# A SwiGLU feed-forward on one core: whole-array matmuls in the opening stage, fewer junk matmuls, and the first weight sums split by matrix

## The chip, the cores and the metric

The kernel runs on 1 core of one Trainium2 chip. The metric is the device time of one execution in microseconds; of several runs the median counts. The profile is that of one execution, whose instructions and DMA packets are given in microseconds from the start of its span.

## What is computed

```python
def reference(x, w_gate, w_up, w_down):
    g = silu(x @ w_gate)
    u = x @ w_up
    return (g * u) @ w_down
```

All tensors are bf16: x is 2048 tokens by D = 512, w_gate and w_up are 512 by F = 1376, w_down is 1376 by 512. F is ten tiles of 128 and a remainder of 96.

## The kernel before

**Stages.** The 2048 tokens are four chunks c of 512. The first stage makes, for each F tile `ft` and chunk, a gate and an up product in PSUM (4 matmuls over D, or 8 of half the columns), takes the silu of the gate on ScalarE and the product h on VectorE. The second multiplies h by w_down. Most of both is done in a Strassen-like scheme: blocks of two F tiles by two chunks (a unit) take 7 instead of 8 block products, on sums of weights (S1 to S4) and sums of x (T1 to T4) that are made ahead, and PSUM results are put together by VectorE and POOL. The rest is "classic": F tiles 0-3 of chunk 0 (lines 688-701), the same tiles of chunk 1 (`early`, lines 1014-1023; F tile 3 at line 1047), and the remainder of F (`plan_x`, `plan_y`, lines 1037-1044).

**Order on TensorE** at the start: 6 warm-up matmuls; transposes of tokens 0-255; junk matmuls (`between`, line 395), which read a constant and write a bank that nothing reads; gates of F tiles 0-3 for tokens 0-511, in pieces as weights and tokens land; ups of these (line 700); the early tiles 0, 1, 2 of tokens 512-1023; then the remainder: `plan_x` for chunks 0 and 1, `plan_y` for both, `plan_x` for chunks 2 and 3, `plan_y`; then the first unit, the early tile 3, and the other units.

**Halves and whole.** `gu_emit` (line 421) issues each step over D as two matmuls, one for each half of 64 columns of the array, side by side. `gu_whole` (line 433) issues it as one of 128 columns. `gu_group` (line 443) and `classic` (line 470) choose: `classic` takes the whole array where banks are handed to it (`own`).

**Loads.** All loads are issued on SP's queue in the order of lines 282-321: x of tokens 0-255 (`xn`), gate weights of F tiles 0-3 (`wg0`, `wg2`), x of tokens 256-511 (`x0b`, a transposing DMA), up weights of F tiles 0-3 (`wu0`, `wu2`), x of tokens 512-767 and 768-1023 (`x1a`, `x1b`, transposing), weights of F tiles 4, 5 and of 8 to the end, x of chunks 2 and 3, weights of 6, 7, and w_down.

**The planner.** Work on TensorE and SP has a fixed order. Work on ScalarE (A), VectorE (D) and POOL (G) is ordered by `Plan.schedule` (lines 59-103): again and again the operation that can start earliest goes next, ties going to the lower priority number. It reckons with costs that are written in the code and, for loads, with dates of landing (`.land`, line 259): the sum of the loads' sizes so far, plus 300 ns where this is under 10000, else plus 1600. Each engine then runs its list in order and waits on semaphores, so an operation that waits holds back those behind it.

**Sums.** `w_sums(0, ...)` (line 1015) makes the weight sums of F tiles 0 and 1 on POOL: four instructions, each for gate and up together, so they wait for both weights. `x_sums(0, "D", ...)` makes T1 to T4 of tokens 0-1023 on VectorE, one behind the other, T1 behind the last of the weight sums; the weight sums of the units follow T4 on POOL.

**Banks.** PSUM has 8 banks. The gates of chunk 0 take 0-3, the ups 4-7; the early tiles take (0, 2), (1, 3), (4, 5); `plan_x` of chunks 0, 1, 2, 3 takes 6, 7, 5, 2; `plan_y` takes 4 and 3. So `plan_x` of chunk 2 waits until the product h of early tile 2 has read bank 5.

Of the kernel before, what the change touches and what calls it, by code (L numbers as in the profile page):

```python
# [5 lines left out]
ALU = mybir.AluOpType  # L6
BF16 = mybir.dt.bfloat16
FP32 = mybir.dt.float32
# [1 line left out]

N_WARM = 6
N_FILL = 1
N_BETWEEN = 5

PE_STEP, PE_STEP4, PE_LAG = 216, 231, 205
A_BUSY, A_LAG = 485, 180
# [152 lines left out]
def bass_standalone__swiglu_ffn__prompt_kernel(nc, x, w_gate, w_up, w_down, out):  # L169
    _, S, D = x.shape  # L170
    F = w_gate.shape[1]
    P = 128
    KD = D // P
    KH = KD // 2
# [3 lines left out]
    SC = 512  # L178
# [6 lines left out]
    HT = SC // 2  # L185
    HC = P // 2
    NXN = HT // P
    NB = 8
# [8 lines left out]
    XC0 = NFF * P  # L197

    with ExitStack() as es:
# [7 lines left out]
        w_sb = sb("w_sb", [P, KD, 2, WW], BF16)  # L207
# [18 lines left out]
        psum = ps("psum", [P, NB, 512], FP32)  # L226
# [19 lines left out]
        ones_w = nc.const_aps.tensor(1.0, [P, P], BF16)  # L246
        ones_m = nc.const_aps.tensor(1.0, [P, SC], BF16)
        zero_c = nc.const_aps.tensor(0.0, [P, 4], FP32)

        plan = Plan()  # L250
        engines = {"P": nc.tensor, "S": nc.sync, "A": nc.scalar, "D": nc.vector, "G": nc.gpsimd}

        landed = 2700

        def load(name, emit, writes, busy, lag):
            nonlocal landed
            landed += lag
            i = take(homes[name] if name in homes else rest[0])
            plan.add("S", emit, writes=writes, busy=busy, lag=1800, dma=(i, 16)).land = landed + (300 if landed < 10000 else 1600)

        slabs = [(0, 2), (2, 4), (4, 6), (6, 8), (8, NFF + 1)]
        slab_of = {ft: a for a, b in slabs for ft in range(a, b)}
# [73 lines left out]
        def tt_op(engs, out, a, b, alu, reads, writes, prio, busy, after=()):  # L336
            return plan.add(
                engs, lambda e: e.tensor_tensor(out, a, b, alu), reads, writes, busy,  # L338
                G_LAG if engs == "G" else D_LAG, prio, after=after,
            )  # L340
# [5 lines left out]
        def pe(emit, reads, writes, n, step=PE_STEP, after=()):  # L346
            return plan.add("P", emit, reads, writes, int(n * step), PE_LAG, dma=None, after=after)
# [37 lines left out]
        for dk in range(KD):  # L385
            keys = [("b", 2 * dk), ("b", 2 * dk + 1)] if dk < KD - 1 else [("b", 6)]
# [6 lines left out]
            copy_op("DA"[dk % 2], out, src, keys, [("x0a", dk)], 0, 300)  # L393

        def between(e):
            for i in range(N_BETWEEN):
                for h in (0, HC):
                    ins = e.matmul(
                        psum[h:h + HC, NB - 1, 0:P], lhsT=ones_w[:, 0:HC], rhs=ones_m[:, 0:P],
                        start=True, stop=True, tile_position=(0, h),  # L400
                    )
            return ins

        pe(between, (), [("b", NB - 1)], N_BETWEEN / 4)

        n_group = 0

        def next_bank():
            nonlocal n_group
            b = turn[n_group % NB]  # L410
            n_group += 1
            return b
# [8 lines left out]
        def gu_emit(m, ft, c, b, dks, n0, n1):  # L421
            def emit(e):
                for dk in dks:
                    for h in (0, HC):
                        ins = e.matmul(  # L425
                            psum[h:h + HC, b, n0:n1], lhsT=w_sb[:, dk, m, ft * P + h:ft * P + h + HC],
                            rhs=xT_sb[:, dk, c * SC + n0:c * SC + n1], start=(dk == 0), stop=(dk == KD - 1),
                            tile_position=(0, h),
                        )
                return ins  # L430
            return emit
# [33 lines left out]
        def classic_out(ft, c, bg, bu):  # L465
            sg, ksg = ring("sg", sg_sb)
            silu_op(sg, bank(bg), [("b", bg)], [ksg])
            tt_op("D", hview(ft, c), sg, bank(bu), ALU.mult, [ksg, ("b", bu)], [("h", ft, c)], 5, D_BUSY)

        def classic(c, fts, own=None):  # L470
            gates = [next_bank() for ft in fts] if own is None else own[:1]
            ups = [next_bank() for ft in fts] if own is None else own[1:]
            for ft, b in zip(fts, gates):
                gu_group(0, ft, c, b, own is not None)
            for ft, b in zip(fts, ups):
                gu_group(1, ft, c, b, own is not None)
            for ft, bg, bu in zip(fts, gates, ups):
                classic_out(ft, c, bg, bu)
# [4 lines left out]
            return (0, 64) if c % 2 == 0 else (64, 128)  # L483

        def plan_x(c, b):
            def emit(e):
                for dk in range(KD):
                    for m in (0, HC):
                        ins = e.matmul(  # L489
                            psum[m:m + HC, b, :], lhsT=w_sb[:, dk, 0, XC0 + m:XC0 + m + HC],  # L490
                            rhs=xT_sb[:, dk, c * SC:(c + 1) * SC],
                            start=(dk == 0), stop=(dk == KD - 1), tile_position=(0, m),
                        )
                return ins
            pe(emit, x_keys(c) + [f"wg{slab_of[NFF]}", "wut"], [("b", b)], KD)
            y0, y1 = yblk(c)
            sgx, kx = sgx_sb[c % 2], ("sgx", c % 2)
            silu_op(sgx[96:128, :], psum[64:96, b, :], [("b", b)], [kx], 4, 610)
            silu_op(sgy_sb[c // 2][y0:y1, :], psum[0:64, b, :], [("b", b)], [("sgy", c)], 4, 610)
            tt_op(  # L500
                "D", htx_sb[R * c:R * (c + 1), :], sgx[96:128, :], psum[96:128, b, :], ALU.mult,
                [kx, ("b", b)], [("htx", c)], 4, D_BUSY,
            )
            if c == LC:
                tt_op(
                    "D", hl_sb[2 * R:3 * R, :], sgx[96:128, SC - P:SC], psum[96:128, b, SC - P:SC], ALU.mult,
                    [kx, ("b", b)], [("hl", 2)], 4, 300,
                )
# [34 lines left out]
                reads, writes, busy, A_LAG if eng == "A" else G_LAG, prio, after=after,  # L543
            )

        def w_sums(u, prio, after, casts):

            f0, f1 = 2 * u * P, (2 * u + 1) * P
            slot = len(slot_of) % NSLOT
            slot_of[u] = slot  # L550
            block = lambda k, f: w_sb[:, k * KH:(k + 1) * KH, :, f:f + P].rearrange("p k m c -> p m k c")
            at = lambda n: ss_sb[:, slot, W_SUM[n], :, :, :]
            keys = lambda n: [("ss", slot, n, m) for m in range(2)]
            wkeys = [f"w{g}{slab_of[2 * u]}" for g in "gu"]
            for n in ("S1", "S2", "S3", "S4"):
                A11, A12, A21, A22 = (block(k, f) for f in (f0, f1) for k in range(2))
                rd = lambda n: at(n).bitcast(FP32)
                a, b, alu, of_ = {
                    "S1": (A21, A22, ALU.add, ()), "S2": (rd("S1"), A11, ALU.subtract, ["S1"]),
                    "S3": (A11, A21, ALU.subtract, ()), "S4": (A12, rd("S2"), ALU.subtract, ["S2"]),  # L560
                }[n]
                last = tt_op("G", at(n), a, b, alu, wkeys + [k for o in of_ for k in keys(o)], keys(n), prio, 1180, after)
            for m in range(2):
                cast_op(
                    casts, at("A22")[:, m], w_sb[:, KH:2 * KH, m, f1:f1 + P], [wkeys[m]], [("ss", slot, "A22", m)], 8, 360,
                    after if casts == "G" else () if slot < 3 else [last],
                )
            return [last]
# [121 lines left out]
        ups = [NB // 2 + ft for ft in first]  # L690
# [6 lines left out]
        for ft in first:  # L697
            pe(gu_emit(0, ft, 0, gates[ft], range(KD), HT, SC), ["x0b", f"wg{slab_of[ft]}"], [("b", gates[ft])], 2)
        for ft in first:
            gu_group(1, ft, 0, ups[ft])  # L700
            classic_out(ft, 0, gates[ft], ups[ft])

        F_ORDER = [ft for u in U_ORDER[1] for ft in (2 * u, 2 * u + 1)]
# [308 lines left out]

        units = [(pi, u) for pi in range(2) for u in U_ORDER[pi]]
        early = [2 * u + i for u in range(NFF // 2) if u not in U_ORDER[0] for i in range(2)]
        sums = w_sums(0, 8, (), "A")
        g, u = next_bank(), next_bank()
        for h in range(2):
            for m, b in ((0, g), (1, u)):
                emit = gu_emit(m, early[0], 1, b, range(KD), h * HT, (h + 1) * HT)
                pe(emit, [f"x1{'ab'[h]}", f"w{'gu'[m]}{slab_of[early[0]]}"], [("b", b)], KD / 2)  # L1020
        classic_out(early[0], 1, g, u)
        for ft in early[1:3]:
            classic(1, [ft])
        sums = x_sums(0, "D", 4, sums)
        for u in U_ORDER[0]:
            sums = w_sums(u, 2, sums, "A")
        sums = x_sums(1, "G", 2, sums)
# [20 lines left out]
        for n in range(len(units)):  # L1048
# [4 lines left out]
            if n + 1 < len(units):  # L1053
                after = make(n + 1)
# [41 lines left out]
```

## Time and profile before

| | us |
|---|---|
| median of the runs | 115.34 |
| lowest and highest of 3 runs | 114.77, 115.77 |
| the profiled execution | 115.92 |
| its span, first to last instruction | 114.6 |

| engine | busy us | share | instructions |
|---|---|---|---|
| PE (TensorE matmuls) | 111.6 | 97% | 692 |
| PEld (weight loads, beside matmuls) | 69.9 | 61% | 692 |
| DVE (VectorE) | 77.0 | 67% | 113 |
| ACT (ScalarE) | 63.6 | 55% | 123 |
| POOL | 61.5 | 54% | 57 |

How to read it: the chain of waits starts at the last instruction and goes back, at each step, to what released it or to the instruction before it on its engine; its rows give start, length and what ran. A timeline row gives start, length, engine, line of the code, operation, what it writes and reads, the shape, and in brackets the idle time before it with what ended that. `DMA x<-y` is the landing of a load. A windows row gives, for one stretch, its length, the busy time and the number of instructions of PE, PEld, DVE, ACT and POOL, the granted TensorE clock, the busy share of the 16 DMA engines and the GB/s that started in it. A share counts each packet with its whole time where it starts, so it can be over 1. Lines such as L338 are helpers that many operations share: what is written (h_sb, tt_sb, ss_sb) tells them apart.

### The profile page before, as it was taken

How to read it: one execution, taken by the hardware profiler on the slowest of the kernel's cores; microseconds unless marked ns; L12 is line 12 of the kernel's file. 1: busy time of each engine (PE TensorE's matmuls, PEld its weight loads, DVE VectorE, ACT ScalarE, POOL GpSimd, SP SyncE). 2: the span in 40 equal slices, each digit the busy share in tenths (PEclk: the TensorE clock that was granted, in tenths of full speed). 3: DMA queues.
4: the chain of work that ended last, by engine and by line, in shares of the span. 5: the costliest groups of instructions: out<-in, count | busy, mean ns of one | idle time of the engine just before them, and what ended most of it. 6: DMA issues, size and time to landing. Idle time of an engine off the chain costs nothing.

```text
span 114.6 us, 1847 instructions
## 1 busy us (share of the span) xinstructions
PE 111.6 (97%) x692; PEld 69.9 (61%) x692; DVE 77.0 (67%) x113; ACT 63.6 (55%) x123; POOL 61.5 (54%) x57
## 2 busy tenths in 40 slices
PE   7999999999999999999999999999999999999993
PEld 2784854446685857677685858654344556866452
DVE  0104799984866839493957769499999957486423
ACT  5344477774878897767678786740576960000000
POOL 1008701999999999997999999975000000000000
DMA  3999999998000000000000000000041002227966
GB/s 85 261 241 105 260 294 245 221 357 232 10 0 0 3 0 3 6 0 0 0 0 0 3 0 0 6 0 0 0 136 46 0 6 46 46 46 182 200 192 205
DMA packets 22809, 9.84 MB, mean 86 GB/s; under 512 B 12849, under 2 KB 22673, under 8 KB 22801
## 3 DMA queue, kind: packets, MB, share of 16 engines
q1 hardware_dynamic: 20656, 8.69, 33.8%
q10 hardware_dynamic: 2144, 1.05, 3.2%
q8 instruction: 5, 0.08, 0.3%
q14 instruction: 4, 0.02, 0.1%
HBM read 4.75 MB, written 2.10 MB: 60 GB/s over the span
## 4 chain that ended last, share of the span: by engine, by line
PE 90%; DMA 4%; SPq 3%; DVE 1%; issue 0%
PE psum L611 32%; PE psum L724 15%; PE psum L623 12%; PE psum L862 10%; PE psum L425 8%; DMA w_sb<-in_w_up_dram 4%; PE psum L874 4%; PE psum L489 3%; PE psum L752 3%; PE psum L515 2%; PE psum L436 2%; SPq L279 1%; SPq L267 1%; DVE o_sb L327 1%; SPq L284 0%
## 5 line engine op out<-in xcount | busy, mean ns | idle before, releaser
L611 PE MATMUL psum<-tt_sb,ss_sb 128*128 128x512 f32 x160 | 40.0, 403 | 0.0
L611 PEld LDWEIGHTS psum<-tt_sb,ss_sb 128*128 128x128 f32 x160 | 29.9, 188 | 7.5 <-DVE psum L327 0.3
L338 DVE TENSOR_TENSOR ts_sb<-r_sb,psum 128x512 f32<-128x512 f32 x32 | 20.6, 682 | 14.7 <-ACT r_sb L326 14.7
L338 POOL TENSOR_TENSOR h_sb<-sg_sb,ts_sb 128x512 bf16<-128x512 f32 x16 | 20.9, 1311 | 2.2 <-ACT sg_sb L333 2.2
L338 DVE TENSOR_TENSOR h_sb<-sg_sb,psum 128x512 bf16<-128x512 f32 x24 | 16.4, 684 | 6.5 <-PE psum L425 6.1
L326 ACT ACTIVATE r_sb<-psum 128x512 f32<-128x512 f32 x32 | 17.3, 596 | 5.4 <-PE psum L611 5.4
L338 POOL TENSOR_TENSOR ss_sb<-w_sb 128x512 fp32r<-128x512 bf16 x10 | 11.4, 1162 | 14.4 <-DMA w_sb<-in_w_up_dram 7.9
L333 ACT ACTIVATE sg_sb<-psum 128x512 f32<-128x512 f32 x24 | 14.1, 600 | 8.2 <-PE psum L611 5.4
L724 PE MATMUL psum<-wd_sb,h_sb 128*128 128x512 bf16 (+2 forms) x100 | 18.4, 337 | 0.0
L623 PE MATMUL psum<-xT_sb,w_sb 128*128 128x512 bf16 x64 | 15.4, 381 | 0.0
L724 PEld LDWEIGHTS psum<-wd_sb,h_sb 128*128 128x128 bf16 x100 | 8.3, 98 | 9.2 <-issue 1.0
L425 PE MATMUL psum<-xT_sb,w_sb 128*64 128x256 bf16 (+1 forms) x160 | 12.7, 319 | 0.2 <-DMA w_sb<-in_w_up_dram 0.2
L333 ACT ACTIVATE sg_sb<-ts_sb 128x512 f32<-128x512 f32 x16 | 10.2, 636 | 2.2 <-DVE ts_sb L338 2.2
L425 PEld LDWEIGHTS psum<-xT_sb,w_sb 128*64 128x64 bf16 x160 | 8.8, 112 | 3.7 <-DMA w_sb<-in_w_up_dram 0.4
L623 PEld LDWEIGHTS psum<-xT_sb,w_sb 128*128 128x128 bf16 x64 | 5.5, 98 | 8.0 <-issue 2.5
L327 DVE COPY psum<-psum 128x512 f32<-128x512 f32 x8 | 5.6, 699 | 0.9 <-PE psum L623 0.2
L338 POOL TENSOR_TENSOR ss_sb<-w_sb,ss_sb 128x512 fp32r<-128x512 bf16 x5 | 5.9, 1171 | 0.2
L338 POOL TENSOR_TENSOR ss_sb<-ss_sb,w_sb 128x512 fp32r<-128x512 f32 x5 | 5.8, 1168 | 0.0
L327 DVE CAST o_sb<-psum 128x512 bf16<-128x512 f32 (+2 forms) x6 | 3.0, 512 | 4.2 <-PE psum L724 3.1
L338 POOL TENSOR_TENSOR ss_sb<-wd_sb 128x640 fp32r<-128x640 bf16 x4 | 5.6, 1427 | 0.0
L862 PE MATMUL psum<-tt_sb,ss_sb 128*128 128x512 f32 x20 | 5.6, 417 | 0.0
L862 PE MATMUL psum<-th_sb,ss_sb 128*128 128x512 f32 x20 | 5.5, 411 | 0.0
(72 smaller groups left out, 122.0 us busy)
## 6 DMA issues: line engine op xcount, KB each, us to landing
wd_sb<-in_w_down_dram SPq DMA_DIRECT2D x1, 1280.0 KB, 9.1
w_sb<-in_w_gate_dram SPq DMA_DIRECT2D x4, 256.0 KB, 3.9
w_sb<-in_w_up_dram SPq DMA_DIRECT2D x4, 256.0 KB, 4.7
out_dram<-o_sb SPq DMA_DIRECT2D x7, 128.0 KB, 1.8
out_dram<-xT_sb ACTq DMA_DIRECT2D x4, 128.0 KB, 2.5
out_dram<-xT_sb ACTq DMA_DIRECT2D x2, 256.0 KB, 3.3
w_sb<-in_w_gate_dram SPq DMA_DIRECT2D x1, 352.0 KB, 4.5
w_sb<-in_w_up_dram SPq DMA_DIRECT2D x1, 320.0 KB, 5.0
```

What stands on the lines that cost most here:

```text
L326: return e.activation(out, src, ACT.Copy)
L327: return e.tensor_copy(out, src)
L333: "A", lambda e: e.activation(out, src, ACT.Silu), reads, writes, busy, A_LAG, prio
L338: engs, lambda e: e.tensor_tensor(out, a, b, alu), reads, writes, busy,
L425: ins = e.matmul(psum[h:h + HC, b, n0:n1], lhsT=w_sb[:, dk, m, ft * P + h:ft * P + h + HC], rhs=xT_sb[:, dk, c * SC + n0:c * SC + n1], sta ...
L489: ins = e.matmul(psum[m:m + HC, b, :], lhsT=w_sb[:, dk, 0, XC0 + m:XC0 + m + HC], rhs=xT_sb[:, dk, c * SC:(c + 1) * SC], start=(dk == 0), ...
L611: ins = e.matmul(bank(dst), lhsT=s[:, k, :], rhs=t[:, k, :], start=(start and k == 0), stop=(k == KH - 1), skip_group_check=True,)
L623: ins = e.matmul(bank(dst), lhsT=w_sb[:, k0 + k, m, f:f + P], rhs=xT_sb[:, k0 + k, c:c + SC], start=(start and k == 0), stop=(k == KH - 1) ...
L724: ins = e.matmul(psum[:, b, 0:c1 - c0], lhsT=hrows(F_ORDER[n], t, 0, P), rhs=wd_sb[:, F_ORDER[n], c0:c1], start=(start and n == n0), stop= ...
L752: ins = e.matmul(bank(b), lhsT=lhsT, rhs=rhs, start=(start and n == 0), stop=(n == 2 and (kind == "T" or not start)), tile_position=(r0, 0 ...
L862: ins = e.matmul(bank(dst), lhsT=self.ds[s][:, j, self.q, :], rhs=self.dt[t][:, j, :], start=(start and n == 0), stop=(n == NFF // 2 - 1), ...
L874: ins = e.matmul(bank(dst), lhsT=wd_sb[:, 2 * j + a, d * P:(d + 1) * P], rhs=h0_sb[:, 2 * j + a, 0:SC], start=(n == 0), stop=(n == NFF // ...
```

## The change

1. The junk between transposes and gates is one pair of 512 columns and one of 128, instead of five pairs of 128.
2. The ups of tokens 0-511 (F tiles 0-3) go on the whole array.
3. The early F tiles 0, 1, 2 of tokens 512-1023 go on the whole array, in the same banks; tile 0 is no longer made in two pieces by `x1a` and `x1b`.
4. `plan_x` is whole for chunks 0 and 1, and by halves as before for chunks 2 and 3.
5. The weight sums of F tiles 0 and 1 are made for gate and for up apart: eight instructions of half the size, those of gate waiting for gate weights alone, with a planned cost of 620 instead of 1180 ns each.
6. The planner's allowance for a landing changes from 300 to 1600 ns at 10500 instead of 10000. The one load between these two is `x1b`, at 10331: it is planned for 10631 instead of 11931.

```diff
-N_BETWEEN = 5
+N_BETWEEN = (512, 128)
...
-... .land = landed + (300 if landed < 10000 else 1600)
+... .land = landed + (300 if landed < 10500 else 1600)
...
-            for i in range(N_BETWEEN):
+            for n in N_BETWEEN:
                 for h in (0, HC):
                     ins = e.matmul(
-                        psum[h:h + HC, NB - 1, 0:P], lhsT=ones_w[:, 0:HC], rhs=ones_m[:, 0:P],
+                        psum[h:h + HC, NB - 1, 0:n], lhsT=ones_w[:, 0:HC], rhs=ones_m[:, 0:n],
...
         def plan_x(c, b):
+            width = P if c < 2 else HC
+
             def emit(e):
                 for dk in range(KD):
-                    for m in (0, HC):
+                    for m in range(0, P, width):
...
+            for ms in ((0, 1), (1, 2)) if apart else ((0, 2),):
+                block = lambda k, f: w_sb[:, k * KH:(k + 1) * KH, ms[0]:ms[1], f:f + P].rearrange("p k m c -> p m k c")
+                part = lambda n: at(n)[:, ms[0]:ms[1]]
...
+                    last = tt_op(
+                        "G", part(n), a, b, alu, reads + [k for o in of_ for k in keys(o)], keys(n), prio,
+                        620 if apart else 1180, after,
+                    )
...
-            gu_group(1, ft, 0, ups[ft])
+            gu_group(1, ft, 0, ups[ft], True)
...
-        sums = w_sums(0, 8, (), "A")
-        g, u = next_bank(), next_bank()
-        for h in range(2):
-            for m, b in ((0, g), (1, u)):
-                emit = gu_emit(m, early[0], 1, b, range(KD), h * HT, (h + 1) * HT)
-                pe(emit, [f"x1{'ab'[h]}", f"w{'gu'[m]}{slab_of[early[0]]}"], [("b", b)], KD / 2)
-        classic_out(early[0], 1, g, u)
-        for ft in early[1:3]:
-            classic(1, [ft])
+        sums = w_sums(0, 8, (), "A", True)
+        for ft in early[:3]:
+            classic(1, [ft], [next_bank(), next_bank()])
```

More of the change, by code (lines that the diff above doesn't have):

```diff
@@ L258, in load @@
             i = take(homes[name] if name in homes else rest[0])
-            plan.add("S", emit, writes=writes, busy=busy, lag=1800, dma=(i, 16)).land = landed + (300 if landed < 10000 else 1600)
+            plan.add("S", emit, writes=writes, busy=busy, lag=1800, dma=(i, 16)).land = landed + (300 if landed < 10500 else 1600)
         slabs = [(0, 2), (2, 4), (4, 6), (6, 8), (8, NFF + 1)]
@@ L402, in between @@
             return ins
-        pe(between, (), [("b", NB - 1)], N_BETWEEN / 4)
+        pe(between, (), [("b", NB - 1)], sum(N_BETWEEN) / SC)
         n_group = 0
@@ L485, in plan_x @@
         def plan_x(c, b):
+            width = P if c < 2 else HC
             def emit(e):
                 for dk in range(KD):
-                    for m in (0, HC):
+                    for m in range(0, P, width):
                         ins = e.matmul(
-                            psum[m:m + HC, b, :], lhsT=w_sb[:, dk, 0, XC0 + m:XC0 + m + HC],
+                            psum[m:m + width, b, :], lhsT=w_sb[:, dk, 0, XC0 + m:XC0 + m + width],
                             rhs=xT_sb[:, dk, c * SC:(c + 1) * SC],
-                            start=(dk == 0), stop=(dk == KD - 1), tile_position=(0, m),
+                            start=(dk == 0), stop=(dk == KD - 1),
+                            tile_position=(0, m) if width < P else None,
                         )
@@ L544, in cast_op, with w_sums @@
             )
-        def w_sums(u, prio, after, casts):
+        def w_sums(u, prio, after, casts, apart=False):
             f0, f1 = 2 * u * P, (2 * u + 1) * P
@@ L550, in w_sums @@
             slot_of[u] = slot
-            block = lambda k, f: w_sb[:, k * KH:(k + 1) * KH, :, f:f + P].rearrange("p k m c -> p m k c")
             at = lambda n: ss_sb[:, slot, W_SUM[n], :, :, :]
[L553 to L562, printed above, removed]
+            wkeys = [[f"w{g}{slab_of[2 * u]}"] for g in "gu"]
@@ new lines, in w_sums @@
+            for ms in ((0, 1), (1, 2)) if apart else ((0, 2),):
+                block = lambda k, f: w_sb[:, k * KH:(k + 1) * KH, ms[0]:ms[1], f:f + P].rearrange("p k m c -> p m k c")
+                part = lambda n: at(n)[:, ms[0]:ms[1]]
+                rd = lambda n: part(n).bitcast(FP32)
+                keys = lambda n: [("ss", slot, n, m) for m in range(*ms)]
+                reads = [k for m in range(*ms) for k in wkeys[m]]
+                for n in ("S1", "S2", "S3", "S4"):
+                    A11, A12, A21, A22 = (block(k, f) for f in (f0, f1) for k in range(2))
+                    a, b, alu, of_ = {
+                        "S1": (A21, A22, ALU.add, ()), "S2": (rd("S1"), A11, ALU.subtract, ["S1"]),
+                        "S3": (A11, A21, ALU.subtract, ()), "S4": (A12, rd("S2"), ALU.subtract, ["S2"]),
+                    }[n]
+                    last = tt_op(
+                        "G", part(n), a, b, alu, reads + [k for o in of_ for k in keys(o)], keys(n), prio,
+                        620 if apart else 1180, after,
+                    )
@@ L563, in w_sums @@
             for m in range(2):
                 cast_op(
-                    casts, at("A22")[:, m], w_sb[:, KH:2 * KH, m, f1:f1 + P], [wkeys[m]], [("ss", slot, "A22", m)], 8, 360,
+                    casts, at("A22")[:, m], w_sb[:, KH:2 * KH, m, f1:f1 + P], wkeys[m], [("ss", slot, "A22", m)], 8, 360,
                     after if casts == "G" else () if slot < 3 else [last],
```

## The prediction

> **What bounds the kernel now.** The page came first, for the shares and for the instruction queue:
>
> ```profile
> span 114.6 us, 1847 instructions
> PE 111.6 (97%) x692; PEld 69.9 (61%) x692; DVE 77.0 (67%) x113; ACT 63.6 (55%) x123; POOL 61.5 (54%) x57
> ...
> q8 instruction: 5, 0.08, 0.3%
> ```
>
> TensorE is busy for 97% of the span, so a change is worth only what it adds to or takes from TensorE's few gaps. The chain of waits, in order of time, shows where they are:
>
> ```profile
> 3.93 4.85 DMA w_sb<-in_w_up_dram
> ...
> 8.83 8.84 PE psum L425 x96
> 17.67 1.73 PE psum L489 x16
> 19.40 0.86 PE psum L515 x8
> 20.26 0.13 issue
> 20.39 1.99 PE psum L489 x16
> ...
> 23.25 0.97 PE psum L623 x4
> 24.22 1.73 PE psum L436 x8
> ...
> 112.04 0.88 DVE o_sb L327 x3
> ```
>
> Until 8.78 the load of the first up weights (issued at 3.93) sets the time; from 8.83 to 112.0 it is TensorE alone. Two things are to be seen. First, 16 matmuls of half a column set (L489) take 1.73 us and 8 whole ones (L436) take 1.73 us: 0.216 us per group of 512 tokens by 128 rows either way. The whole array saves no TensorE time; it saves instructions. Second, between 17.67 and the end of the remainder tiles the same 16 matmuls cost 1.99 us the second time, behind 0.13 us of idling: 0.13 + 0.26 = 0.39 us is all that waits take in this stretch.
>
> Next the DMA engines, by windows (the last two columns are their busy share and GB/s):
>
> ```profile
> 9.45:10.33 0.88, 0.88 (x11) 0.45 (x8) 0.33 (x1) 0.31 (x2) 0.88 (x2) 1.00 1.32 292
> 10.34:11.05 0.71, 0.71 (x10) 0.38 (x8) 0.54 (x2) 0.00 (x0) 0.71 (x1) 1.00 1.87 13
> 11.08:11.83 0.75, 0.75 (x10) 0.39 (x8) 0.58 (x2) 0.00 (x0) 0.75 (x2) 1.00 0.08 10
> 11.85:12.70 0.85, 0.85 (x14) 0.58 (x12) 0.68 (x2) 0.00 (x0) 0.77 (x2) 1.00 1.24 314
> 22.97:23.89 0.92, 0.92 (x8) 0.36 (x5) 0.65 (x2) 0.90 (x3) 0.84 (x2) 1.00 1.01 328
> ```
>
> The rate falls from 292 GB/s to 13, then 10, and is back at 314 from 11.85: a hole of 1.5 us (10.34 to 11.85) in the middle of x1b, the transposing load of tokens 768-1023. In its second half the share is 0.08, about one engine of 16. The DMA view of the stretch 9.88 to 9.90 shows what went ahead of it:
>
> ```profile
> q8 instruction: 1, 0.02, 366.9%
> ```
>
> One 16 KB packet of the instruction queue starts there, and the share gives its length: 3.669 x 0.02 us x 16 engines is 1.17 us, to 11.07, where the trickle of one engine begins. I read it so: one engine fetches instructions, falls behind with its part of the transpose, and the others wait until it has caught up. The last window is the second fetch, at 22.96, with plain loads in flight: 328 GB/s, no hole.
>
> Whose instructions they are, the counts in the stretches between fetches tell (counts of PE and PEld in brackets):
>
> ```profile
> 0.00:9.89 9.89, 8.95 (x108) 6.02 (x110) 0.73 (x3) 4.93 (x10) 1.40 (x6) 1.00 0.95 185
> 9.89:22.96 13.07, 12.94 (x136) 7.29 (x132) 11.86 (x15) 7.78 (x16) 6.83 (x7) 1.00 1.17 236
> ...
> 73.26:93.65 20.39, 20.39 (x124) 9.92 (x123) 19.70 (x23) 12.84 (x25) 4.79 (x4) 1.00 0.08 27
> 93.65:108.90 15.25, 15.25 (x69) 9.85 (x69) 8.94 (x14) 0.00 (x0) 0.00 (x0) 1.00 0.45 99
> ```
>
> 218, 268 and 247 TensorE instructions: some 250 to a fetch, on TensorE's progress and not on time.
>
> **The change, part by part.** Edits that shorten TensorE's instruction stream go together: 6 junk matmuls fewer (10 to 4), 16 in the ups of tokens 0-511, 24 in the first early tile (32 to 8), 16 in the next two, 8 in the remainder tiles of tokens 0-1023. That is 70 matmuls, and with a weight load each 140 instructions. Directly they are worth almost nothing: 0.216 us per group stays, and the junk has 640 columns before and after (five times 128; 512 + 128), so its 0.54 us (4.25 to the gates at 4.79) stays. The first row below shows the cover for the junk: TensorE stands idle for 0.17 us until the up weights land. Without that idling each tenth there would cost a tenth.
>
> ```profile
> 8.83 0.41 PE L425 MATMUL psum<-xT_sb,w_sb 128*64 128x512 bf16 x2 [0.17 <-DMA w_sb<-in_w_up_dram]
> 8.82:12.30 3.48, 3.47 (x32) 1.80 (x34) 1.96 (x3) 0.94 (x3) 3.37 (x3) 1.00 1.05 123
> ```
>
> Indirectly they move the first fetch. It came at 218 instructions, in the ups. In the changed stream 12 go ahead of the ups and the ups issue 32 instead of the last row's 66, so 218 is reached only at the end of the ups, near 12.3, where TensorE first has to get past its wait for x1b. If so, x1b lands before the fetch.
>
> The first early tile now wants all of x1 at once; before, its first half ran on x1a alone. When x1b lands decides what that costs:
>
> ```profile
> L279 SPq DMA_TRANSPOSE xT_sb<-in_x_dram x1: 2006/2006/2006, 7.5 to 7.5; - x1
> ...
> DMA to landing us min/median/max: 5.5/5.5/5.5
> 13.09 1.15 ACT L542 ACTIVATE tt_sb<-xT_sb 128x512 fp32r<-128x512 bf16 x2 [3.33 <-DMA xT_sb<-in_x_dram]
> ```
>
> Now it lands at 7.5 + 5.5 = 13.0 (ScalarE, waiting for it, starts at 13.09). TensorE ends the ups at 8.83 + 16 x 0.216 = 12.3. So the bounds of this edit are 0.75 us of new waiting (landing unchanged) and none (landing 1.5 us earlier, at 11.5). I take none, because the hole begins inside the fetch and its trickle starts when the fetch ends; both ends stay in the range.
>
> The sums of F tiles 0 and 1 by halves: 8 instructions of 256 columns for 4 of 512 on POOL.
>
> ```profile
> L338 POOL TENSOR_TENSOR ss_sb<-w_sb 128x512 fp32r<-128x512 bf16 x10 | 11.4, 1162 | 14.4 <-DMA w_sb<-in_w_up_dram 7.9 <-DVE tt_sb L338 6.2 <-POOL ss_sb L338 0.3
> L338 POOL TENSOR_TENSOR ss_sb<-wd_sb 128x640 fp32r<-128x640 bf16 x4 | 5.6, 1427 | 0.0
> 12.40 1.17 POOL L338 TENSOR_TENSOR ss_sb<-w_sb,ss_sb 128x512 fp32r<-128x512 bf16 x1
> 13.70 1.22 DVE L338 TENSOR_TENSOR tt_sb<-xT_sb 128x1024 fp32r<-128x1024 bf16 x1 [0.43 <-POOL ss_sb L338]
> ```
>
> 128 columns more cost 0.265 us, so 256 cost about 1.162 - 0.53 = 0.63 us (estimate from these two rows; bounds 0.58, half, and 1.16). The four for gate run while POOL waits for up (7.9 us), the four for up end near 8.93 + 4 x 0.63 = 11.5 instead of 13.57. VectorE's first x sum (T1, at 13.70) is then released by x1b alone: 2.1 us earlier at the best.
>
> The planner's earlier date for x1b (10.63 instead of 11.93 us on its own clock) reorders VectorE. By its rule (earliest start, then priority) T1 now comes ahead of the products h of F tiles 2 and 3, whose ups it dates 11.21 and 12.08: h0, h1, T1, h2, T2, h3, T3, then the early products and T4. SP's queue holds the same loads in the same order. POOL's sums for the units follow T4 as before and, with T4 no later (19.5 even with x1b at 13.0, 19.6 now), come no later. With x1b at 11.5 T1 runs at about 11.6 and the later products are in time; with x1b at 13.0 h2 and h3 stand behind it.
>
> What VectorE is worth to TensorE, and its pace, are in these rows (those that write tt_sb are T sums):
>
> ```profile
> 16.10 0.68 DVE L338 TENSOR_TENSOR h_sb<-sg_sb,psum 128x512 bf16<-128x512 f32 x1
> 16.70 1.22 DVE L338 TENSOR_TENSOR tt_sb<-xT_sb 128x1024 fp32r<-128x1024 bf16 x1
> 17.83 0.68 DVE L338 TENSOR_TENSOR h_sb<-sg_sb,psum 128x512 bf16<-128x512 f32 x1
> 19.56 0.68 DVE L338 TENSOR_TENSOR h_sb<-sg_sb,psum 128x512 bf16<-128x512 f32 x1
> 20.28 0.69 DVE L338 TENSOR_TENSOR htx_sb<-sgx_sb,psum 32x512 bf16<-32x512 f32 x1
> ```
>
> A T sum holds VectorE for 1.13 us (16.70 to 17.83), a product behind which a sum comes 0.60, another 0.72. The product of 19.56 frees bank 5 at 20.24, and TensorE's third remainder tile (20.39) waited for that: the 0.13 us above. The other 0.26 are mostly refilling and the wait for the last x load, of tokens 1536-2047:
>
> ```profile
> 21.33 0.57 PEld L489 LDWEIGHTS psum<-xT_sb,w_sb 128*64 128x64 bf16 x8 [0.36 <-DMA xT_sb<-in_x_dram]
> ```
>
> With T1 at 11.6 that product ends near 11.6 + 4 x 1.13 + 3 x 0.60 + 0.72 + 0.68 = 19.3 at the latest, before TensorE needs bank 5 at about 20.1: the 0.39 us go, if the last x load too is 0.3 us earlier. Its queue loses a hole of 1.5 and gains a fetch of 1.17 elsewhere, so 0.3 is what I expect; with no change there the gain is about 0.
>
> One cost is new: the remainder tiles of tokens 0-1023 are whole, the next are halves. The chain has a change from halves to whole at 23.25: 0.97 us for 4 groups worth 0.86, so 0.11 us a change. I take 0.11; bounds 0 and 0.2. The same change ahead of the ups lies in the idle 0.17 us.
>
> **Sum.** -0.39 + 0.11 = -0.28, say -0.25 because the last x load may still hold some. The profiled execution took 115.92 us (span 114.6), 0.58 over the median of the runs, 115.34; I take the difference to be the same in both: 115.7 profiled, 115.1 for the median. About 1%, 1.15 us, is what a measurement of this kernel can tell from no change, so this is "the same".
>
> **Rivals.**
>
> x1b does not come earlier (slower). The fetch is not what holds it, or comes as early as before. For: an earlier stretch of low rate (8.15 to 9.43, below) has no instruction packet. Against: the fit of fetch and trickle.
>
> ```profile
> 8.15:9.43 1.28, 1.11 (x16) 0.61 (x14) 0.00 (x0) 1.28 (x4) 0.50 (x1) 1.00 1.25 50
> ```
>
> TensorE then waits 0.75 us at 12.3. T1 starts at 13.1, and with the same paces the product that frees bank 5 ends at 13.1 + 4 x 1.13 + 3 x 0.60 + 0.72 + 0.68 = 20.8; TensorE goes on 0.15 later, at 20.97 instead of 20.39: +0.58, of which the last x load (now early enough) gives 0.04 back. 115.34 + 0.54 = 115.9. It decides from x1b landing past 12.3; over 13.6 it would be more than 1%.
> The Trainium skill, page "Runtime: NRT & Kernel Launch", section "Instruction fetch mechanics", says that a boundary of 16 KiB (256 instructions) costs "one DMA tail-bump, mostly hidden". By that rule no fetch holds a load and this rival comes out, 115.9; the count of 250 agrees with the page, the hole at 10.34 speaks against "hidden", the window at 22.97 for it.
>
> The last fetch meets the stores. It moves from 93.65, in quiet, by 138 instructions (the row 93.65 to 108.90) to about 109, where the last output transposes are in flight. A hole like the first (1.2 to 1.5 us) holds the stores that ScalarE's queue issues behind them:
>
> ```profile
> 109.72 1.76 ACTq L712 DMA_DIRECT2D out_dram<-xT_sb  x3
> ...
> DMA to landing us min/median/max: 1.9/2.2/2.7
> ```
>
> The last of the three is issued by 111.5 and, 2.7 us from its start at about 111.0, has landed by 113.7; the span ends at 114.6. Of 1.2 to 1.5 us, 0.3 to 0.6 would show: about 115.5 with the gain above.
>
> No part matters: last x load unmoved, hidden fetch at both places: 115.3.
>
> **How the numbers follow.** x1b early, 0.60 (115.1); x1b late, 0.18 (115.9); late stores, 0.10 (115.5); nothing, 0.12 (115.3). The runs of before spread from 114.77 to 115.77, so half a microsecond lies around each. Range 114.5 to 116.2: the gain in full with a fast sample below, the late x1b with its 0.3 of spread above. Slower by over 1% needs x1b still later than now, 0.09; faster by over 1% needs more than all the gaps named, 0.06; the same, 0.85.
>
> **What would show it.** 622 matmuls; the first instruction packet at 11.5 or later; no hole before x1b lands, by 12.3; no wait of TensorE at 12.3 and none on the product at 20.1; POOL's sums from 4.5. A wait of PE on the x load near 12.3, or a 16 KB packet before 10, would prove me wrong; so would a last store held by a transpose.

## The result and the profile after

The changed kernel took 116.68 us (median of six executions, 116.21 to 117.12), the kernel before 115.28 beside it: a ratio of 1.0117, 95% interval 1.0076 to 1.0159. A second measurement (e13 below) gave 1.0079, 1.0052 to 1.0106. It is slower by about 1%, 0.9 to 1.4 us; the forecast of 115.1, range 114.5 to 116.2, missed it. The profiled execution took 116.9 us, its span is 115.6: 1.0 more than the span before.

The page after:

```profile
span 115.6 us, 1700 instructions
...
PE 111.0 (96%) x613; PEld 68.3 (59%) x622; DVE 76.6 (66%) x113; ACT 63.8 (55%) x123; POOL 62.2 (54%) x61
...
q8 instruction: 5, 0.08, 0.3%
```

622 weight loads are there as forecast (nine matmul records of 622 are missing from the trace, which leaves holes of about 0.2 us that the chain calls "issue"). There are still five instruction packets. The chain of waits after, in order of time:

```profile
9.12 0.16 issue
9.28 8.69 PE psum L436 x39
17.96 1.73 PE psum L491 x8
19.69 0.98 PE psum L518 x8
20.68 1.73 PE psum L491 x16
22.40 0.86 PE psum L518 x8
...
25.96 2.85 PE psum L620 x12
...
112.08 0.88 DVE o_sb L327 x3
```

The first unit begins at 25.96; in the kernel before it was this row of its chain:

```profile
25.94 2.88 PE psum L611 x12
```

The third remainder group now takes 1.73 us with no idling ahead of it: the 0.39 us of waits are gone. The gain is used up ahead of that: TensorE starts the ups at about 9.06 (with a missing record filled in) instead of 8.83, waits 0.11 us for `x1b`, and the row at 19.69 is 0.12 us longer. So the units start at the same time, and VectorE's last piece ends at 112.96 as it ended at 112.92. In this pair of profiles the front and the long middle are equal; the whole difference lies behind VectorE's last piece, 115.6 - 112.96 = 2.64 us against 114.6 - 112.92 = 1.68.

What is there is output traffic. The windows around 109.4 to 110.4 us, first of before, then of after:

```profile
109.40:109.90 0.50, 0.50 (x4) 0.26 (x3) 0.00 (x0) 0.00 (x0) 0.00 (x0) 1.00 0.32 70
109.90:110.40 0.50, 0.50 (x5) 0.25 (x4) 0.15 (x1) 0.00 (x0) 0.00 (x0) 1.00 0.96 318
```

```profile
109.40:109.90 0.50, 0.50 (x4) 0.22 (x3) 0.00 (x0) 0.00 (x0) 0.00 (x0) 1.00 1.42 22
109.90:110.40 0.50, 0.50 (x4) 0.27 (x3) 0.11 (x1) 0.00 (x0) 0.00 (x0) 1.00 0.08 9
```

70 and 318 GB/s have become 22 and 9, with a share of 0.08 at the end: the picture of the first fetch in the kernel before. The DMA view of the stretch 108.92 to 108.94 shows the packet ahead of it:

```profile
q8 instruction: 1, 0.02, 289.1%
```

2.891 x 0.02 x 16 = 0.93 us, from 108.93 on. It was at 93.65. In flight are the last output transposes on SP's queue (L901 before, L910 after). Their issue to landing, and that of the last two stores of `o_sb`, before:

```profile
L901 SPq DMA_TRANSPOSE xT_sb<-xT_sb x3: 1276/1314/2106, 103.8 to 106.5; - x3
...
DMA to landing us min/median/max: 2.8/3.5/4.5
```

```profile
L712 SPq DMA_DIRECT2D out_dram<-o_sb x2: 332/382/432, 112.6 to 113.0; - x2
DMA to landing us min/median/max: 1.6/1.6/1.6
```

and after:

```profile
L910 SPq DMA_TRANSPOSE xT_sb<-xT_sb x3: 1276/1307/2084, 103.8 to 106.5; - x3
...
DMA to landing us min/median/max: 2.8/4.8/5.9
```

```profile
L721 SPq DMA_DIRECT2D out_dram<-o_sb x2: 333/433/533, 112.7 to 113.0; - x2
DMA to landing us min/median/max: 2.3/2.3/2.3
```

The transposes are issued at the same times and land 1.4 us later. ScalarE's queue issues three stores behind them, at 111.16 to 112.43 instead of 109.72 to 110.98, and these run into the last stores of SP, which land 2.3 us after issue instead of 1.6. This is the rival "The last fetch meets the stores", at the place that was forecast.

### The profile page after: what moved, and what is told of

It is laid out like the page before. It is cut to its first block, busy times and chain, and to the rows that moved or that the text cites. A ratio compares the mean times of both kernels' runs of the same rounds, so it can differ in the third digit from the quotient of the medians.

```text
span 115.6 us, 1700 instructions
## 1 busy us (share of the span) xinstructions
PE 111.0 (96%) x613; PEld 68.3 (59%) x622; DVE 76.6 (66%) x113; ACT 63.8 (55%) x123; POOL 62.2 (54%) x61
## 4 chain that ended last, share of the span: by engine, by line
PE 96%; issue 1%; DVE 1%
PE psum L620 32%; PE psum L733 14%; PE psum L632 12%; PE psum L871 10%; PE psum L436 9%; PE psum L883 4%; PE psum L425 4%; PE psum L491 3%; PE psum L761 3%; PE psum L351 2%; PE psum L518 2%; DVE o_sb L327 1%; PE psum L398 0%; PE psum L374 0%; PE psum L381 0%
## 5 line engine op out<-in xcount | busy, mean ns | idle before, releaser
L338 POOL TENSOR_TENSOR ss_sb<-w_sb 128x512 fp32r<-128x512 bf16 (+1 forms) x12 | 11.7, 996 | 13.1 <-DVE tt_sb L338 8.1
L733 PE MATMUL psum<-wd_sb,h_sb 128*128 128x512 bf16 (+2 forms) x98 | 17.9, 336 | 0.2 <-issue 0.2
L632 PE MATMUL psum<-xT_sb,w_sb 128*128 128x512 bf16 x59 | 14.2, 380 | 0.4 <-issue 0.2
L436 PE MATMUL psum<-xT_sb,w_sb 128*128 128x512 bf16 x47 | 10.6, 379 | 0.2 <-issue 0.2
L632 PEld LDWEIGHTS psum<-xT_sb,w_sb 128*128 128x128 bf16 x64 | 5.5, 98 | 8.0 <-issue 2.5
L436 PEld LDWEIGHTS psum<-xT_sb,w_sb 128*128 128x128 bf16 x48 | 4.5, 97 | 5.8 <-issue 0.6
L338 POOL TENSOR_TENSOR ss_sb<-w_sb,ss_sb 128x512 fp32r<-128x512 bf16 (+1 forms) x6 | 6.0, 1008 | 0.3
L338 POOL TENSOR_TENSOR ss_sb<-ss_sb,w_sb 128x512 fp32r<-128x512 f32 (+1 forms) x6 | 6.0, 998 | 0.0
```

The lines of the kernel that those rows point to most:

```text
L436: ins = e.matmul(bank(b), lhsT=w_sb[:, dk, m, ft * P:(ft + 1) * P], rhs=xT_sb[:, dk, c * SC:(c + 1) * SC], start=(dk == 0), stop=(dk == KD ...
L632: ins = e.matmul(bank(dst), lhsT=w_sb[:, k0 + k, m, f:f + P], rhs=xT_sb[:, k0 + k, c:c + SC], start=(start and k == 0), stop=(k == KH - 1) ...
L733: ins = e.matmul(psum[:, b, 0:c1 - c0], lhsT=hrows(F_ORDER[n], t, 0, P), rhs=wd_sb[:, F_ORDER[n], c0:c1], start=(start and n == n0), stop= ...
```

## The experiments

The theory: the last fetch is moved into the output transposes by the 140 PE instructions that went. Rivals: the front of the kernel is later, by the junk pairs (J), the sums apart and VectorE's order (S), or the whole-array form itself (W).

One measure separates tail from front in a single profile: the time from the end of TensorE's last matmul to the landing of the last store. The kernels that differ in the number of instructions, on that measure:

| kernel | PE instructions fewer than before | last fetch at | slowest of the last two transposes, issue to landing | last store behind TensorE | ratio to before (95%) |
|---|---|---|---|---|---|
| before | 0 | 93.65 | 4.5 | 1.90 | 1 |
| e10 | 12 | 92.62 | 4.5 | 1.90 | 1.0004 (0.9981 to 1.0027) |
| e2 | 12 | 93.10 | 4.5 | 1.90 | 1.0027 (1.0002 to 1.0051) |
| e12 | 60 | 99.88 | 4.4 | 1.90 | 1.0036 (1.0017 to 1.0055) |
| e11 | 104 | 103.77 | 3.7 | 1.91 | 1.0038 (1.0017 to 1.0059) |
| e3 | 128 | 105.94 | 5.4 | 2.35 | 1.0053 (1.0030 to 1.0077) |
| after | 140 | 108.93 | 5.9 | 2.69 | 1.0117 (1.0076 to 1.0159) |
| e13 (after again) | 140 | 108.44 | 5.9 | 2.66 | 1.0079 (1.0052 to 1.0106) |
| e1 | 156 | 109.17 | 5.3 | 2.19 | 1.0078 (1.0047 to 1.0108) |
| e9 | 192 | 88.63, the fourth | 4.5 | 1.91 | 1.0016 (0.9989 to 1.0043) |
| e7 | 192 | 89.08, the fourth | 4.5 | 1.90 | 1.0048 (1.0021 to 1.0075) |
| e6 | 204 | 89.16, the fourth | 4.5 | 1.91 | 1.0023 (1.0001 to 1.0046) |

e8 and e14 to e18, with as many instructions as the kernel before, have their last fetch at 92.8 to 93.8 and a tail of 1.90 or 1.91. In every profile with five packets the last one comes when 1148 to 1175 of TensorE's recorded matmuls and loads have begun (1173 before, 1160 after). The three kernels with four packets have 1192 and 1180 of them in all. So the date goes with the count.

**e1: sixteen instructions fewer still.**

```diff
-            width = P if c < 2 else HC
+            width = P
```

> The changed kernel with the x-sum product of chunks 2 and 3 on the whole array as well: 8 matmuls and 8 weight loads fewer, nothing else. Theory (the last instruction fetch, at 108.93 us in the changed kernel, holds the output transposes of the last x bar): 16 PE instructions fewer move it behind them or out of the program; the two output transposes land near 109.65 and 109.94 as in the kernel before, the ACT stores are issued near 109.7, and the time is 115.3 to 115.8. Rival (the front, longer cold by the new junk pairs, or the whole-array form itself): nothing of these 16 instructions bears on it, 116.5 to 116.9.

116.31 us, 1.0078. The fetch moved by 0.24 us only, to 109.17: my expectation that it would leave the transposes failed. The first of the two was not held (4.5 us), only the second (5.3); the tail is 2.19 us, between the quiet one and the late one. The rivals, by which these 16 instructions change nothing, do not fit either: the tail is 0.5 us shorter, and the time lies between the two forecasts. This form has also two more changes between whole array and halves, about 0.1 us each.

**e2: everything but the whole-array form.** The kernel after, with all matmuls of the kernel before.

```diff
-            gu_group(1, ft, 0, ups[ft], True)
+            gu_group(1, ft, 0, ups[ft])
```

and likewise for the early tiles and `plan_x`.

> The kernel before with two junk pairs for five, the sums apart and the new landing date, but all matmuls by halves: 12 PE instructions fewer than the kernel before. Theory (late fetch): the last fetch stays in a quiet stretch, near 95 us, output transposes land near 109.7 and the time is 115.1 to 115.5. Rival (the front is later by the junk pairs): about 116.5. Rival (the waits at px2 and px3 were worth their 0.39 us): 114.9.

115.67 us: quiet tail, as the theory has it, but 0.2 us above its range, and a remaining 0.3% that it does not explain. The rivals of 116.5 and of 114.9 are out.

**e3: the whole-array form alone.** The kernel before with the three whole-array edits of the diff.

> The kernel before with the whole-array form alone (ups of chunk 0, early tiles and x-sum product of chunk 1): 128 PE instructions fewer, five junk pairs, old sums and old landing date. Theory (late fetch): the last fetch comes near 107.6 us, while the output transposes are under way, and the time is 116.2 to 116.8, as the whole change. Rival (the junk pairs make it slower): 115.1 to 115.4.

116.19 us; the fetch at 105.94 holds the last two transposes (5.4 and 4.2 us for 4.5 and 3.5), the tail is 2.35. The time is at the lower edge of the theory's range, and the mechanism is the theory's.

**e6: more whole-array matmuls, so that the fifth fetch goes.** The kernel after, its gates of tokens 0-511 by one matmul of 128 columns each, where `gu_emit` issues two.

```diff
-                pe(gu_emit(0, ft, 0, gates[ft], [dk], 0, HT), ...
+                pe(gu_part(0, ft, 0, gates[ft], [dk], 0, HT), ...
```

> The changed kernel with the gates of tokens 0 to 511 on the whole array too: 32 matmuls and 32 weight loads fewer. Theory (fetches decide): the last fetch is out of the program or behind the output transposes, these land near 109.7; the first one comes behind the start of the early tiles (11 us or later), so that x1b lands near 11.2 instead of 12.5; 114.6 to 115.4. Rival (the front or the whole array makes the change slow): 116.5 or more.

The page of e6, and its output transposes:

```profile
span 114.5 us, 1636 instructions
...
q8 instruction: 4, 0.07, 0.2%
```

```profile
L920 SPq DMA_TRANSPOSE xT_sb<-xT_sb x3: 1277/1316/2080, 103.7 to 106.4; - x3
...
DMA to landing us min/median/max: 2.8/3.4/4.5
```

Four packets, no fetch in the tail, transposes as in the kernel before: 115.78 us, above the 115.4 that I had put as the highest. It has more of the whole-array form than the changed kernel and its ratio is 1.0023 (1.0001 to 1.0046) against 1.0117 and 1.0079, so W is not the main part of what made the change slow. The first fetch too came where the prediction had wanted it, at 13.66 us, and `x1b` landed at 10.44. In this profile it brought nothing: the units start at 25.90 in its chain.

```profile
9.32 8.58 PE psum L446 x39
...
25.90 2.87 PE psum L630 x12
```

**e7, e8, e9, e10: what the remaining 0.2 to 0.3% is.** e7 is e6 with `N_BETWEEN = (128,) * 5`; e8 is the kernel before with the sums apart and the new landing date alone; e9 is e3 with e6's gates; e10 is the kernel before with the junk edit alone.

> e6 (the changed kernel with the gates of chunk 0 on the whole array) with five junk pairs of 128 columns again for 512 + 128: 6 matmuls and 6 loads more than e6. e6 has a quiet tail (its last store lands 1.91 us behind TensorE's last matmul, as in the kernel before) and is still 0.2% slower than the kernel before. Theory J (the two junk pairs let the tensor clock rise later): 115.2 to 115.4, and the 256-column gate steps fall from 0.213 to 0.109 us before 5.3 us in the profile. Theory S (the sums apart or their order cost it) or theory W (the whole-array form does): as e6, ratio near 1.0025, 115.7.

> The kernel before with the sums of F tiles 0, 1 apart and the new landing date alone: five junk pairs, every matmul by halves, the PE instructions of the kernel before. The waits of 0.39 us at the x-sum products of chunks 2 and 3 go, the tail stays quiet. Theory J (junk pairs) and theory W (whole array): no cost left, 115.0 to 115.4. Theory S (sums apart): as e2, ratio near 1.0025, 115.7.

> Whole-array form everywhere that e6 has it (gates and ups of chunk 0, early tiles, x-sum product of chunk 1), but with five junk pairs, the sums together and the old landing date: 192 PE instructions fewer than the kernel before. Late-fetch theory: the last fetch is out of the tail, and its transposes land 3.4 to 4.6 us after their issue. Theory J and theory S: 115.2 to 115.4. Theory W: as e6, 115.7.

> The kernel before with two junk pairs (512 + 128 columns) for five of 128 and nothing else: 12 PE instructions fewer. Theory J: slower, ratio near 1.0025, 115.7, and the gate steps fall to 0.109 us later than 5.3 us in the profile. Theories S and W: no change, 115.3 to 115.5. The tail stays quiet in all of them.

e7 115.88 (1.0048), e8 115.55 (1.0021, 0.9996 to 1.0046), e9 115.75 (1.0016), e10 115.46 (1.0004). J falls twice: five pairs did not help e7, two pairs do not hurt e10. e7 has a quiet tail and is 0.5% slower all the same, with an interval (1.0021 to 1.0075) that leaves out 1: the late fetch is not the whole of it. S and W both stay possible at about 0.2%.

**e11, e12, e13: the instruction count alone.** e11 is the changed kernel with 36 instructions more, in the warm-up only:

```diff
-                e.matmul(bank(NB - 1), lhsT=ones_w, rhs=ones_m, start=True, stop=True)
+                for k in range(0, SC, P):
+                    e.matmul(psum[:, NB - 1, k:k + P], lhsT=ones_w, rhs=ones_m[:, k:k + P], start=True, stop=True)
```

e12 is the changed kernel with the early tiles by halves, e13 the changed kernel itself, all on one chip.

> The changed kernel with each of its six warm-up matmuls of 512 columns cut into four of 128: the same columns, 18 matmuls and 18 weight loads more, all ahead of the first gate. The front and every later form are the changed kernel's. Late-fetch theory: 36 PE instructions more bring the last fetch from 108.9 to about 103 us (0.11 us for an instruction, as between e2 with 93.1 and e3 with 105.9), behind which the last two output transposes are yet to be issued; they land within 4.6 us of issue, the last store lands 1.9 to 2.2 us behind TensorE's last matmul (2.69 in the changed kernel), 115.6 to 116.0. Rival (forms and sums make the change slow, not the fetch): 116.4 to 116.8.

> The changed kernel with the three early F tiles by halves as in the kernel before: 40 matmuls and 40 weight loads more. Late-fetch theory: 80 instructions more bring the last fetch to 98 to 100 us, ahead of the output transposes of the last chunk; last store 1.90 us behind TensorE's last matmul, 115.5 to 115.9. Rival (the ups on the whole array or the sums apart cost the time): 116.4 to 116.8.

> The changed kernel itself, beside the other two on one chip. Late-fetch theory: the last fetch comes near 109 us again in its profile, the last two output transposes land 5 to 6 us after issue, the last store 2.2 to 2.8 us behind TensorE's last matmul, and the ratio is 1.008 to 1.012, more than that of the other two kernels of this call by 0.005 or more. If the first measurement was a chance of the chip: ratio near 1.003.

The output transposes of e13 and of e11:

```profile
L910 SPq DMA_TRANSPOSE xT_sb<-xT_sb x3: 1276/1307/2042, 103.3 to 106.0; - x3
...
DMA to landing us min/median/max: 2.8/4.8/5.9
```

```profile
L911 SPq DMA_TRANSPOSE xT_sb<-xT_sb x3: 1307/1553/2291, 103.9 to 107.6; - x3
...
DMA to landing us min/median/max: 3.1/3.7/3.8
```

e13 repeats the changed kernel's tail. In e11, which computes and orders the same with the same forms, the fetch at 103.77 holds the transposes before them; the last two are issued 1.1 us later (the last at 107.58) but land in 3.1 and 3.7, the last store is 1.91 us behind TensorE, and the time is 115.91. The last transpose lands as late as in the changed kernel (111.30 and 111.32); it is the first of the two that lands earlier, at 109.38 instead of 111.09, and with it ScalarE's first store goes out at 109.46 instead of 111.16. e12: 115.84. The ratios of both are 0.4% below e13's; I had put 0.5% or more. The medians differ by 0.35 and 0.42 us; the means of e13 and e11 differ by 0.50, with a 95% interval of 0.18 to 0.83 reckoned from their executions. The tail differs by 2.66 - 1.91 = 0.75 us in the profiles, which lies within it.

**e14, e15, e16, e17, e18: is it POOL's early work (P), or VectorE's order (D)?** In most of the profiles so far TensorE's gate steps went from 0.213 to 0.109 us later where the sums are apart (not in e13 and e8). e14 is e8 with

```diff
-                reads = [k for m in range(*ms) for k in wkeys[m]]
+                reads = wkeys[0] + wkeys[1]
```

e15 is the kernel before with four idle sums on POOL, e16 the kernel before again, e17 e8 again, e18 e8 with the old landing date.

> e8 (the kernel before with the sums apart and the new landing date) with the gate sums waiting for the up weights too, so that POOL does nothing between 2 and 8 us. Theory P (POOL's early work delays the tensor clock): ratio 1.000, 115.3, gate steps fall to 0.109 us by 5.2 us. Theory chance: as e8, ratio 1.002, any moment from 4.4 to 6.5 us.

> The kernel before with four more sums of 256 columns on POOL as soon as the gate weights land (about 4.5 to 7.2 us); nothing waits for them and their result is overwritten. Theory P: ratio 1.003 or more, 115.7, gate steps fall to 0.109 us later than 5.3 us. Theory chance: ratio 1.000, 115.3.

> The kernel before, for a second profile. Theory P: the gate steps fall to 0.109 us by 5.3 us. Tail of 1.90 us behind TensorE's last matmul under every theory; 114.8 to 115.9.

> e8 again, beside e14 on one chip. Theory P: ratio 1.002 to 1.004 and above e14's, gate steps fall to 0.109 us at 5.1 us or later. Theory chance: the ratio of e14.

> The kernel before with the sums apart alone and the old landing date: VectorE's order is three products, T1, a product, T2 instead of two products, T1, a product, T2, a product (e8). Theory D (the order by the new date costs the 0.2 to 0.3%): ratio 1.000, 115.3. Theory S (the sums apart as such, eight instructions for four): ratio 1.0025, 115.6. An interval that holds both leaves it open.

e14 115.61 (1.0027, 0.9995 to 1.0060), e15 115.30 (1.0005, 0.9981 to 1.0029), e16 115.47 (one execution), e17 115.59 (1.0028, 1.0000 to 1.0055), e18 115.74 (1.0016, 0.9993 to 1.0039). P falls: e16, with POOL idle until the up weights land, changed its steps at 5.87 us only, where P had 5.3 at the latest, and e15 with POOL at work is not slower. (In e15 and e17 the steps are short from the first gate on, at 4.55 and 4.79; POOL began at 4.49 and 4.47.) The four measurements with the sums apart alone lie between 0.16 and 0.28%, but e18's interval holds both D and S. Whether the order, the eight instructions or something else costs that is open.

No version was faster than the kernel before.

## Why the prediction was wrong

**That the whole array saves no TensorE time: right.** From the first unit (25.94, 25.96) to VectorE's last piece nothing moved, and 0.216 us per group stayed.

**The first fetch: wrong.** I had taken 218 instructions executed as its trigger and forecast 11.5 us or later; it came at 9.43. The counts up to it are 218 before and 93 + 95 = 188 after:

```profile
0.00:9.43 9.43, 8.50 (x93) 5.77 (x95) 0.73 (x3) 4.14 (x9) 4.02 (x11) 1.00 0.97 196
9.43:9.95 0.52, 0.52 (x4) 0.22 (x3) 0.00 (x0) 0.52 (x2) 0.52 (x2) 1.00 4.13 249
9.95:10.60 0.65, 0.65 (x5) 0.29 (x4) 0.40 (x1) 0.27 (x1) 0.57 (x2) 1.00 0.16 6
10.60:11.30 0.70, 0.70 (x5) 0.34 (x4) 0.53 (x2) 0.00 (x0) 0.53 (x1) 1.00 0.09 11
11.30:12.60 1.30, 1.30 (x7) 0.42 (x6) 0.45 (x1) 0.02 (x1) 0.00 (x0) 1.00 1.21 300
```

In these two profiles it starts 0.23 to 0.24 us after the second up weights land (9.65 and 9.89; 9.20 and 9.43). That landing is not what starts it: in the second profiles of the same two kernels, e16 and e13, it comes 0.86 and 0.88 us after it (8.63 and 9.49; 8.53 and 9.41). Nor is there a fixed count of executed instructions: these two have 214 and 196, and the 18 profiles have 164 to 218. A count of the instructions issued, which run ahead of those executed by a varying number, would fit; this was not tested by itself. So the hole stayed (6 and 11 GB/s), and `x1b` landed at 12.49, not 11.5.

**What that step was worth: little.** TensorE's wait at the early tile was 0.11 us here and 0.39 in e13. In e6 the fetch was out of the way and the units began no earlier. The late-`x1b` rival, with 0.75 us of waiting, had too much of it.

**The gain of 0.39 us: it was no term of the median.** It went, as forecast. But the second profile of the kernel before (e16) does not have those waits, with nothing changed, and the second profile of the sums apart (e17) has one:

```profile
17.63 1.73 PE psum L489 x16
19.36 0.86 PE psum L515 x8
20.22 1.73 PE psum L489 x16
```

```profile
18.59 1.21 DVE h_sb L338 x2
19.80 0.14 issue
19.94 1.92 PE psum L491 x16
```

A wait that comes and goes between executions of one kernel had been booked as saved, and subtracted from the median, though the execution that showed it was 0.58 us slower than the median. In e10 they are absent too, and it is not faster than the kernel before.

**The change between halves and whole: right in size, one too few.** 19.69 takes 0.98 for 0.86: 0.12, where I took 0.11. A second stands ahead of the ups. I had put it into the idle 0.17 us behind the up weights, but these landed at 8.38, before the gates ended at 9.12, so the cover was gone; of the gap there 0.11 us is left when one missing record is filled in. The Trainium skill, page "TensorEngine Tiling (Array Packing)", section "Key Properties", says that switching the tiling mode drains TensorE; these rows agree and give the price, about 0.1 us. e9 has these changes too and measured 1.0016.

**The late stores: the step that failed.** The date was worked out correctly (about 109; 108.93), and the length of the hole as well (1.2 to 1.5 us; the transposes land 1.4 later). Two errors were made with it. It was put among the rivals at 0.10, though it followed from a count that the forecast itself relied on: it belonged in the sum. And 0.3 to 0.6 us is less than both profiles show: it was reckoned on ScalarE's three stores alone, which end at 115.22, while the stores of SP's queue, crowded by them, land last, at 115.38. The tail grew by 2.69 - 1.90 = 0.79 us, 0.76 in e13. Behind the last landing SP still steps through its closing waits for the stores: the span ends 0.19 us after it in both, 0.04 before. From TensorE's last matmul to the end of the span that makes 2.88 and 2.85 us against 1.95, so 0.93 and 0.90 more. By the executions the size is less certain: e13 against e11 gives 0.50 (0.18 to 0.83), and 0.3 to 0.6 lies within that too.

**The account.** Put right from the profiles, the sum is 115.3, no gain, two changes of 0.1 and 0.8 to 0.9 for the late stores: 116.3 to 116.4 as an estimate, where 116.68 and 116.26 were measured. That the late fetch costs time is shown, by e11 against e13 above all; its size is 0.2 to 0.8 us by the executions and 0.9 by the profiles. A remainder is open. With a quiet tail and some of the other edits, e2, e6, e7, e11 and e12 still are 0.2 to 0.5% slower than the kernel before. Taken singly, the sums apart give 0.2 to 0.3% (e8, e14, e17, with the new date) and 0.16% (e18, without), the whole-array form 0.16% (e9), the junk 0.04% (e10), each with an interval that holds no change, or ends at it (e17). e1 fits least: its tail is 0.29 us longer, its median 0.87. By the profiles, what remains lies ahead of the units, since the stretch from there to TensorE's end is the same in all of them (last section); the units' first matmul starts at 24.25 us (e10) to 25.67 (e7), so a single profile of each cannot resolve it.

The Trainium skill, page "Runtime: NRT & Kernel Launch", section "Instruction fetch mechanics", calls the cost of such a boundary "mostly hidden". That agrees with the fetches at 92.6 to 99.9 us and at 103.77 (tail 1.90 and 1.91), and not with those at 105.94 to 109.17 (2.19 to 2.69): in these runs it depends on which transfer is in flight, and on whether anything waits behind it.

## What to carry to other kernels

Count the instructions of an engine as a schedule of fetches: where an edit changes the count, work out where every later fetch goes, the last one above all, and book a fetch that lands on transposing transfers at the end as a term of the sum. Take a wait for a gain only if it is there in more than one execution; of two profiles of the kernel before, only one had the waits that this forecast wanted to save. If instructions go, a few more or fewer in a place where they cost nothing, such as a warm-up, can move a fetch off a transfer.

## What the hardware showed

The fetch does not stop TensorE, which went on without a gap at 108.9; what slows down is a transposing DMA. Plain loads in flight at 22.96 kept 328 GB/s, transposes fell to 6 to 22. How much is lost varies: the output transpose in flight at the fetches of e10 (92.62) and e17 (93.34) landed 2.8 and 2.9 us after issue, where others of its size took 2.4, and nothing waited for it.

The moment when TensorE's steps go from 0.213 to 0.109 us lay between 4.17 us or earlier (e13) and 6.59 us (e18), whatever the kernel, while the granted clock in the rows reads 1.00 throughout. The same kernel twice, junk (4 matmuls) and gates of tokens 0-511 (64 matmuls), after and e13:

```profile
4.23 0.75 PE L398 MATMUL psum<-const-bfloat16-1.0 128*64 128x512 bf16 x4
4.76 4.36 PE L425 MATMUL psum<-xT_sb,w_sb 128*64 128x256 bf16 x64
```

```profile
4.17 0.44 PE L398 MATMUL psum<-const-bfloat16-1.0 128*64 128x512 bf16 x4
4.50 3.85 PE L425 MATMUL psum<-xT_sb,w_sb 128*64 128x256 bf16 x64
```

In e13 even the junk has the short step. The gates differ by 0.51 us between two executions of one program, as much as most terms of this study. It sits in the front alone: from the first unit's f32 matmul to TensorE's end all profiles take 87.0 to 87.1 us. The Trainium skill, page "TensorE: Matmul & The Clock Gate", section "Part 1: The HAM clock gate", puts the change at around 4 us into sustained work, give or take 0.5, and explains the spread by a window that runs free; here it came from 3.4 us or less to 5.8 us after the first matmul (0.77), a spread of at least 2.4.
